# Order of loads, key rests and probabilities at the start of a causal attention, and two weight blocks placed behind query trips

## The chip, the core and the metric

The kernel runs on one core of one Trainium2 chip. The metric is device time in microseconds (us). Five engines work side by side, each on its own instruction queue: TensorE (PE in the profile, with its weight loads as PEld), VectorE (DVE), ScalarE (ACT), GpSimd (POOL) and SyncE (SP), which here only issues DMA transfers.

## What is computed

Three layers in a row, all in float32:

```python
scores = scale * np.matmul(q, k.transpose(0, 1, 3, 2))       # 2 batches, 12 heads, 448 x 64
mask = np.triu(np.ones((seq, seq), dtype=bool), k=1)
scores = np.where(mask, -1000000000.0, scores)
scores = scores - np.max(scores, axis=-1, keepdims=True)
attn = np.exp(scores)
attn = attn / (np.sum(attn, axis=-1, keepdims=True) + 1e-09)
x = np.matmul(attn, v)                                        # to (896, 768)
h = np.maximum(x @ w_in, 0.0)                                 # 768 x 2048
x = h * h @ w_out                                             # 2048 x 768
expert_idx = np.argmax(logits, axis=1)                        # 8 experts, by cosine
for e in range(E):
    h = np.maximum(x[mask] @ w1[e], 0.0)
    out[mask] = gate_w[mask, None] * (h @ w2[e])
```

## The kernel before

**Precision.** Each float32 operand of a matmul is split into a rounded half ("hi", cast to a 32-bit matmul type) and the rest ("lo", original minus hi). A product is three matmuls: hi x hi, hi x lo, lo x hi. So each key tile k becomes `kh` and `kl`, queries become `q` (both halves side by side), v becomes `vh` and `vl`, and each weight block its own pair. The helpers are `copy_on` (L60, L62: a cast on ACT, DVE or GpSimd) and `lo_of` (L67: the subtraction).

**Attention by pairs.** 24 heads are 12 pairs ("units" in the code, two heads on the 128 partitions). For a pair:

- `s_load` (L164) loads raw queries and keys, 448 KB, into one of three buffers `qk`; pair 0 in two halves. `load_v` (L174) loads v, 256 KB, into one of two buffers.
- `s_prep` (L179) makes `kh` (DVE), `kl` (GpSimd; for pair 0 DVE, by `u0`), and the scaled queries' halves: ACT rounds, DVE takes the rest (L191). For pair 0 they are written straight to where the matmul reads them. For all others they go to a buffer `qs` and from there by two DMAs of 224 KB (L202, one per head) into a block-diagonal layout `q0` or `q1`, whose zeros GpSimd wrote once. This DMA from on-chip memory to on-chip memory is called a **query trip** here. PE can't begin a pair's scores before its trip has landed.
- `s_scores` (L212): seven row blocks c of 64 query rows (both heads: 128 rows), with (c + 1) x 64 keys each; DVE takes the negative maximum, ACT the exponential with its row sum. The scores go through four PSUM banks in turn.
- `s_norm` (L246): reciprocal of the row sums on DVE (L251), then seven products p <- p x rs on GpSimd (L255).
- `s_trans` (L265): PE transposes p (L272, into `pt`), ACT rounds, DVE takes the rest. `s_pv` (L281): p times v, 24 matmuls (L290).
- `s_prep_v` (L204): v's halves; the rounding on ACT for even pairs, on GpSimd for odd, the rest on GpSimd.

**What sets the order.** The main loop (`for k in range(-3, 2 * NU + 2)`, L408) runs by half pairs: scores of the next pair, transposes of the current, products with v of the last. Its text sets PE's order, by `products` (L380), inside a manual section (`man_a`, L407, L428 to L431). GpSimd's setup (masks, zeros) is a manual section too (`zeros`, L70 to L158): it all comes ahead of any other GpSimd work. On the other engines a list scheduler of the framework places each instruction; `tc.issue_after(x)` forces an instruction behind another one in this order, as `w_load` (L106) does for the blocks of w_in, behind the load of v of pair 5 (`rpin`). Every DMA but the gathers is issued by SP, in one queue, and an issue that waits for a buffer or a result holds up all behind it. `warm` (L352) puts a few matmuls without use in front.

**After attention**: w_in and w_out in 16 blocks of 768 KB each (raw 64-bit values, converted on DVE, ACT and GpSimd in `w_load`), routing, and the experts, whose weights are loaded by index. Their code is not touched by the change.

Of the kernel before, what the change touches and what calls it, by code (L numbers as in the profile page):

```python
# [13 lines left out]
ALU = mybir.AluOpType  # L14
# [14 lines left out]
SCALE = 1.0 / 8.0  # L29
# [3 lines left out]
def f32(ap):  # L33
    return ap.bitcast(F32)
# [5 lines left out]
    turn2=[1, 3], ft0=[(0, 3), (1, 3), (2, 3), (3, 3), (4, 3)], ft1=[4], ft2=[3, 5, 6, 7], late=[(2, 5), (3, 5)], ew=[2, 4, 10, 10, 10, 12, 14], stop=0, mlo="V", xh="A", h2="A",  # L40
    wh="G", wil="G", wol="GV", warm=8, nsa=6, nwi=3, nwb=3, wo0=4, hs0=[4, 5, 8, 9], conv0=17, convs=2, pin=1,
    qsb=2, pb=2, ptb=2, qkraw=3, vraw=2, vb=2, ss=4, pts=2, pvs=2, pas=4, wsp=1,
    man=(2, 21),
    ch=(((2, 0, 1), (3,), ()), ((6,), (4, 5), ())), wn=[3, 2, 2], qh="A", qdir=1, qss=2, rpin=5, qdma="SS", kh="V",
    vh="AG", kl="G", vl="G", pth="AAAA", nrm="GGGGGGG", u0=1, order=[2, 1, 3, 0, 4], pm=1,
    pc=dict(D=(1.4, 0.8), S=(1.0, 1.0), M=(1.0, 1.7), T=(0.5, 0.65)))
# [2 lines left out]
def build(tc, qkd, vd, w_in, w_out, emb, tau, wm, cst, out, dbg_y=None):  # L49
# [56 lines left out]
    def w_load(src, f, slot, name, wh="wh", wl="wl", parts=1):  # L106

        pool, sl = slot
        hi = pool.tile([P, DM], F32R, tag=f"s{sl}h", name=name + "h")
        lo = pool.tile([P, DM], F32R, tag=f"s{sl}l", name=name + "l")  # L110
        raw = spool.tile([P, DM, 2], I32, tag="raw", name="raw")
        with tc.issue_after(last.get(("load", CFG["rpin"]), last["load"]).ins):
            DMA.dma_start(out=raw.rearrange("p a b -> p (a b)"), in_=src[:, f, :].bitcast(I32))
        w = spool.tile([P, DM], I32, tag="w24", name="w24")
        n = DM // parts
        for i in range(parts):
            x = slice(i * n, (i + 1) * n)
# [24 lines left out]
    maskf = apool.tile([P, S], F32, name="maskf")  # L142
    tri = cpool.tile([P, P], BF16, name="tri")

    for i in range(2):
        G.memset(f32(qz[i][0:D, :, 1]), 0.0)
        G.memset(f32(qz[i][D:P, :, 0]), 0.0)
        for c in range(0, NQ, 2):
            G.memset(pz[i][c][:, (c + 1) * QC:], 0.0)
        if i == 0:  # L150
            G.memset(maskf[:, 0:S - QC], 0.0)
            G.tensor_copy(maskf[:, S - QC:], mask)
    for x in vz[0] + vz[1]:
        G.memset(f32(x[:, :, 1]), 0.0)
    G.memset(tri, 1.0)
    G.affine_select(out=tri, in_=tri, pattern=[[1, P]], compare_op=ALU.is_gt, fill=0.0, base=0,
                    channel_multiplier=-1)
    zeros.__exit__(None, None, None)  # L158

    def ab(key, u):  # L160
        x = CFG[key]
        return ENG[x[units.index(u) % len(x)]]

    def s_load(u):  # L164
        b, pr = u
        qk = apool.tile([P, 2, S], F32, tag="qk", bufs=CFG["qkraw"], name="qk")
        if u == units[0]:
            for i in range(2):
                DMA.dma_start(out=qk[:, i], in_=qkd[b, pr, :, i])
        else:  # L170
            DMA.dma_start(out=qk, in_=qkd[b, pr])
        st[u] = dict(q=qk[:, 0], k=qk[:, 1])

    def load_v(u):  # L174
        b, pr = u
        st[u]["v"] = v = apool.tile([P, NB, P], F32, tag="v", bufs=CFG["vraw"], name="v")
        last["load"] = last["load", units.index(u)] = DMA.dma_start(out=v, in_=vd[b, pr])

    def s_prep(u):  # L179

        d = st[u]
        for x in ("kh", "kl"):
            d[x] = apool.tile([P, S], F32R, tag=x, bufs=CFG["qsb"], name=x)
        d["q2"] = qz[units.index(u) % len(qz)]
        first = u == units[0] and CFG["u0"]
        kh = copy_on(V if first else ab("kh", u), d["kh"], d["k"])

        def split(r, hi, lo):
            q = d["q"][r].rearrange("p (c a) -> p c a", a=QC)
            copy_on(ENG[CFG["qh"]], hi, q, scale=SCALE)  # L190
            V.scalar_tensor_tensor(out=lo, in0=q, scalar=SCALE, in1=f32(hi), op0=ALU.mult, op1=ALU.subtract)  # L191

        heads = [slice(h * D, (h + 1) * D) for h in range(2)]
        if units.index(u) < CFG["qdir"]:
# [51 lines left out]
    def s_norm(u, cs):  # L246
        d = st[u]
        rs = d["rs"]
        x = slice(COL[cs[0]], COL[cs[-1]] + 1)
        (V if units.index(u) < CFG["pm"] else G).tensor_scalar(out=rs[:, x], in0=d["sm"][:, x], scalar1=1.0e-9, scalar2=None, op0=ALU.add)  # L250
        V.reciprocal(rs[:, x], rs[:, x])  # L251
        for c in cs:
            p = d["p"][c][:, :(c + 1) * QC]
            if CFG["nrm"][c] == "G":
                G.tensor_scalar(out=p, in0=p, scalar1=rs[:, COL[c]:COL[c] + 1], scalar2=1.0, op0=ALU.mult, op1=ALU.mult)  # L255
# [92 lines left out]
    wz = apool.tile([P, 512], BF16, name="wz")
# [55 lines left out]
            mix(run, ("t", 3))  # L404
            mix(run, ("s", 3))

    man_a = tc.manual_schedule(engines={mybir.EngineType.PE})  # L407
    for k in range(-3, 2 * NU + 2):  # L408
        u, h = divmod(k, 2)
        if k == -2:  # L410
            with tc.issue_after(last["q"].ins):
                load_v(units[1])
                s_load(units[3])
        elif h == 0:
            if u + 4 < NU:
# [12 lines left out]
        if k == CFG["man"][0]:  # L428
            man_a.__enter__()
        if k == CFG["man"][1]:  # L430
# [912 lines left out]
```

## Time and profile before

| | |
|---|---|
| time, median of 3 runs (lowest, highest) | 567.44 us (566.59, 568.01) |
| time of the profiled execution | 569.09 us |
| its span, first to last instruction | 567.4 us |
| busy: PE, DVE, ACT, GpSimd | 542.6 (96%), 398.6 (70%), 288.9 (51%), 180.1 (32%) us |
| mean granted clock of TensorE | 0.986 |
| attention's share | the first 112 us or so |

A row of a timeline gives the start, the duration, the engine, the line of the code, the operation, the tile written and the tiles read (buffer numbers left out), the shape, how many of it follow one another, and in brackets how long the engine had been idle before it and for whom. The granted clock is a share of full speed.

### The profile page before, as it was taken

The page shows a single profiled execution, that of the slowest core. Times are in us where ns is not written, and L with a number is a line of the kernel's source. Part 1 is how long each engine was busy: PE and PEld are TensorE (multiplying, and loading weights), DVE is VectorE, ACT ScalarE, POOL GpSimd, SP SyncE. Part 2 cuts the span into 40 slices and gives each one's busy share as a digit, 9 for nine tenths or more (in the row PEclk, how much of TensorE's full clock was granted, in tenths as well). Part 3 has the DMA queues.
Part 4 walks back from the last instruction along what each step waited for, and adds up shares of the span by engine and source line. Part 5 has one row for each costly group of instructions (what it writes and reads, how often), then busy time and mean ns, then how long its engine had stood idle before and what let it go on. Part 6 is the DMA issues. An engine that isn't in the chain of part 4 may idle for free.

```text
span 567.4 us, 9637 instructions
## 1 busy us (share of the span) xinstructions
PE 542.6 (96%) x3429; PEld 506.5 (89%) x3430; DVE 398.6 (70%) x956; ACT 288.9 (51%) x638; POOL 180.1 (32%) x228
## 2 busy tenths in 40 slices
PE   6798899999999999999999999999999999999993
PEld 3698899988999999999899999989998898899992
DVE  6688689943977978597753556898186898783641
ACT  4687688623344433423432234741285897764641
POOL 6787588873555544221000001000301201200010
PEclk9799899999999999999999999999999999999997
DMA  6659454413454655441100006701968879874310
GB/s 169 187 136 253 110 121 100 125 62 112 123 192 137 215 161 182 162 166 57 57 28 1 29 28 245 285 28 57 328 203 280 283 252 365 283 253 155 110 53 5
DMA packets 28234, 86.52 MB, mean 152 GB/s; under 512 B 2822, under 2 KB 13062, under 8 KB 28176
## 3 DMA queue, kind: packets, MB, share of 16 engines
q1 hardware_dynamic: 26640, 79.51, 44.1%
q0 software_dynamic: 1536, 6.29, 3.1%
q8 instruction: 29, 0.48, 0.3%
q14 instruction: 29, 0.24, 0.1%
HBM read 75.24 MB, written 6.29 MB: 144 GB/s over the span
## 4 chain that ended last, share of the span: by engine, by line
PE 84%; DVE 7%; DMA 3%; ACT 3%; POOL 1%; issue 1%; SPq 0%; POOLq 0%; DVEq 0%; ACTq 0%
PE yps L581 19%; PE ops L951 10%; PE pa L314 7%; PE pa L316 7%; PE pa L315 7%; PE pv L290 5%; PE s L229 4%; PE hps L852 3%; PE pt L272 3%; PE ops L889 2%; PE ops L884 2%; DMA q<-qs 2%; PE hps L870 2%; PE hps L872 2%; PE hps L871 2%; DVE ml L67 2%
## 5 line engine op out<-in xcount | busy, mean ns | idle before, releaser
L67 DVE TENSOR_TENSOR ml<-xraw,mh 128x768 fp32r<-128x768 f32 x64 | 59.6, 956 | 10.3 <-ACT mh L60 9.8
L60 ACT ACTIVATE mh<-xraw 128x768 fp32r<-128x768 f32 x64 | 52.2, 843 | 7.6 <-PE ops L884 5.8
L951 PE MATMUL ops<-mh,act 128*128 128x384 f32 x224 | 53.5, 341 | 0.0
L229 PE MATMUL s<-kh,q 128*128 128x128 f32 (+6 forms) x168 | 45.3, 317 | 6.5 <-DMA q<-qs 5.3
L290 PE MATMUL pv<-pt,v 128*128 128x448 f32 (+7 forms) x288 | 49.0, 304 | 0.7 <-ACT pt L60 0.6
L242 ACT ACTIVATE p<-s,mn 128x192 f32<-128x192 f32 (+6 forms) x84 | 39.8, 479 | 18.1 <-DVE mn L239 12.5
L255 POOL TENSOR_SCALAR p<-p,rs 128x192 f32<-128x192 f32 (+6 forms) x84 | 43.6, 539 | 3.7 <-DVE rs L251 3.7
L122 DVE SCALAR_TENSOR_TENSOR w<-raw,w 128x768 int32<-128x768 int32 x32 | 41.9, 1310 | 0.7
L290 PEld LDWEIGHTS pv<-pt,v 128*128 128x128 f32 (+1 forms) x288 | 39.7, 169 | 2.8 <-ACT pt L60 0.8
L977 POOL DMA_INDIRECT out<-osb,fsi x10 | 9.9, 990 | 98.4 <-ACT osb L972 65.9
L239 DVE CUSTOM_DVE_ANT_0 s<-s,maskf 128x192 f32<-128x192 f32 (+6 forms) x77 | 32.4, 432 | 12.2 <-PE s L229 10.5
L229 PEld LDWEIGHTS s<-kh,q 128*128 128x128 f32 x168 | 32.1, 208 | 9.0 <-issue 5.0
L951 PEld LDWEIGHTS ops<-mh,act 128*128 128x128 f32 x224 | 39.2, 188 | 0.8
L67 DVE TENSOR_TENSOR pt<-pt 128x512 fp32r<-128x512 f32 x48 | 32.1, 683 | 9.6 <-ACT pt L60 9.6
L67 DVE TENSOR_TENSOR hs<-h,hs 128x512 fp32r<-128x512 f32 (+1 forms) x32 | 21.8, 690 | 23.1 <-ACT hs L60 22.9
L989 POOL DMA_INDIRECT xr<-ydram,fgi x10 | 10.5, 1052 | 85.4 <-DVE fsi L697 45.5
L120 DVE SCALAR_TENSOR_TENSOR w<-raw,w 128x768 int32<-128x768 int32 x32 | 37.1, 1161 | 0.7
L67 DVE TENSOR_TENSOR ml<-mraw,mh 128x768 fp32r<-128x768 f32 x32 | 29.8, 954 | 10.2 <-ACT mh L60 9.8
L320 ACT ACTIVATE relu<-pa 128x448 f32<-128x448 f32 x32 | 17.0, 539 | 34.3 <-PE pa L316 34.3
L60 ACT ACTIVATE pt<-pt 128x512 fp32r<-128x512 f32 x48 | 28.5, 600 | 11.6 <-PE pt L272 11.4
L272 PE MATMUL pt<-ident,p 128*128 128x128 f32 x192 | 29.9, 286 | 3.5 <-POOL p L255 3.0
L118 DVE TENSOR_SCALAR w<-raw 128x768 int32<-128x768 int32 x32 | 22.5, 704 | 13.8 <-POOL wi3l L67 4.3
(462 smaller groups left out, 1638.6 us busy)
## 6 DMA issues: line engine op xcount, KB each, us to landing
xraw<-in_wm SPq DMA_DIRECT2D x32, 768.0 KB, 5.8
raw<-in_w_in SPq DMA_DIRECT2D x16, 768.0 KB, 4.2
raw<-in_w_out SPq DMA_DIRECT2D x16, 768.0 KB, 4.2
mraw<-in_wm SPq DMA_DIRECT2D x16, 768.0 KB, 5.5
qk<-in_qkd SPq DMA_DIRECT2D x11, 448.0 KB, 5.7
q<-qs SPq DMA_DIRECT2D x22, 224.0 KB, 3.8
v<-in_vd SPq DMA_DIRECT2D x12, 256.0 KB, 3.3
ydram<-ysb SPq DMA_DIRECT2D x7, 384.0 KB, 2.3
```

Of the source, the lines that this page charges most:

```text
L60: return A.activation(out, in_, AF.Copy, scale=scale)
L67: return eng.tensor_tensor(out=lo, in0=x, in1=hi, op=ALU.subtract)
L122: V.scalar_tensor_tensor(out=w[:, x], in0=raw[:, x, 0], scalar=29, in1=w[:, x], op0=ALU.logical_shift_right, op1=ALU.bitwise_or)
L229: T.matmul(ss, d["q2"][:, c, :, :, x].rearrange("p a b -> p (a b)"), d[y][:, :n], start=i_ == 0, stop=i_ == 2 and not first)
L242: last["exp", units.index(u), c] = A.activation(d["p"][c][:, :n], ss, AF.Exp, bias=mn, scale=1.0 if first else -1.0, accum_out=d["sm"][:, ...
L255: G.tensor_scalar(out=p, in0=p, scalar1=rs[:, COL[c]:COL[c] + 1], scalar2=1.0, op0=ALU.mult, op1=ALU.mult)
L272: T.transpose(pt[:, o * P:(o + 1) * P], d["p"][c][:, j * P:(j + 1) * P], ident)
L290: T.matmul(d["pv"][:, j * P:S] if h else d["pv"][0:D, j * P:S], d[x][:, j, 1:3].rearrange("p a b -> p (a b)") if h else d[x][:, j, 0], pt[ ...
L314: T.matmul(ps, wh[:, c], xhi[:, kc, gs], start=(kc == 0), stop=False)
L315: T.matmul(ps, wh[:, c], xlo[:, kc, gs], start=False, stop=False)
L581: T.matmul(ps[t][c][:, :384], x, w[:, c * 384:(c + 1) * 384], start=(f == 0 and w is wh and x is hi), stop=(f == NF - 1 and x is lo))
L951: T.matmul(ps[c], x, ww[:, c * 384:(c + 1) * 384], start=(fc == 0 and x is hh and ww is wh), stop=(fc == 7 and x is hl))
```

## The change

- `hold` is new: a memset of one column of the load's target on DVE, placed behind a given instruction. The load has to follow it. v of pair 0 and the load of pair 2 are held in this way behind the cast of pair 0's keys.
- Pair 0's `kl` goes to GpSimd as all others', and the `u0` exception for keys is gone. Of pair 1, the cast `kh` comes behind the rest of its queries.
- GpSimd's setup is cut in pieces: only pair 0's zeroed query buffer stands ahead of pair 0's `kl`; the zeros of p, the mask and pair 1's query buffer come behind it, then pair 1's `kl`, then the zeros of v, more zeros of p, and `tri` (used much later).
- v of a pair is split behind the last normalization of an earlier half pair (`last["norm", ...]`), so pair 1's v comes behind pair 0's p.
- From pair 4 on a key load is issued behind the last query trip. Block f of w_in is issued behind the trip of pair 6 + f, not behind v of pair 5.
- PE's manual section opens at the start; PE's order in attention is the same as before.

```diff
-    man=(2, 21),
+    man=21,
...
+    man_a = tc.manual_schedule(engines={mybir.EngineType.PE})
+    man_a.__enter__()
...
-        with tc.issue_after(last.get(("load", CFG["rpin"]), last["load"]).ins):
+        pin = last.get(("q", 6 + f)) if src is w_in else None
+        with tc.issue_after((pin or last["load"]).ins):
             DMA.dma_start(out=raw.rearrange("p a b -> p (a b)"), in_=src[:, f, :].bitcast(I32))
...
+    def hold(x, behind):
+
+        if behind is not None:
+            with tc.issue_after(behind.ins):
+                V.memset(x, 0.0)
...
         qk = apool.tile([P, 2, S], F32, tag="qk", bufs=CFG["qkraw"], name="qk")
+        hold(qk[:, 0, 0:1], behind)
...
         st[u]["v"] = v = apool.tile([P, NB, P], F32, tag="v", bufs=CFG["vraw"], name="v")
+        hold(v[:, 0, 0:1], behind)
...
-        first = u == units[0] and CFG["u0"]
-        kh = copy_on(V if first else ab("kh", u), d["kh"], d["k"])
+        i = units.index(u)
+
+        def round_k():
+            last["kh"] = copy_on(ab("kh", u), d["kh"], d["k"])
+
+        if i != 1:
+            round_k()
...
-            split(slice(0, P), q[:, :, :, 0], q[:, :, :, 1])
+            lo = split(slice(0, P), q[:, :, :, 0], q[:, :, :, 1])
+            if i == 1:
+                with tc.issue_after(lo.ins):
+                    round_k()
...
-        lo_of(V if first else ab("kl", u), d["kl"], d["k"], f32(d["kh"]))
+        lo_of(ab("kl", u), d["kl"], d["k"], f32(d["kh"]))
...
     s_load(units[0])
     s_load(units[1])
-    load_v(units[0])
-    s_load(units[2])
     s_prep(units[0])
+    load_v(units[0], last["kh"])
+    s_load(units[2], last["kh"])
+    zero_p(0)
+    G.memset(maskf[:, 0:S - QC], 0.0)
+    G.tensor_copy(maskf[:, S - QC:], mask)
+    zero_q(1)
...
             if u + 4 < NU:
-                s_load(units[u + 4])
+                with tc.issue_after(last["q"].ins):
+                    s_load(units[u + 4])
...
         if h == 1 and 0 <= u + 1 < NU:
-            with tc.issue_after(last["max", 0, 5].ins), tc.issue_after(last["exp", 0, 5].ins):
+            with (tc.issue_after(last["max", 0, 5].ins), tc.issue_after(last["exp", 0, 5].ins),
+                  tc.issue_after(last["norm", max(k - 2, -1)].ins)):
                 s_prep_v(units[u + 1])
```

**Where instructions stand: the first DMA issues.** SP's queue from its start, before and then changed; `qk` are raw queries and keys, `q_108` and `q_110` take pair 1's trip, `q_107` and `q_109` pair 2's.

```order
L169 DMA qk<-in_qkd 128x448 x2
L171 DMA qk<-in_qkd 128x896
L177 DMA v<-in_vd 128x512
L171 DMA qk<-in_qkd 128x896
L202 DMA q_108<-qs 64x7x128 x2
L177 DMA v<-in_vd 128x512
L171 DMA qk<-in_qkd 128x896 x2
L202 DMA q_107<-qs 64x7x128 x2
```

```order
L174 DMA qk<-in_qkd 128x448 x2
L176 DMA qk<-in_qkd 128x896
L183 DMA v<-in_vd 128x512
L176 DMA qk<-in_qkd 128x896
L216 DMA q_110<-qs 64x7x128 x2
L183 DMA v<-in_vd 128x512
L176 DMA qk<-in_qkd 128x896
L216 DMA q_109<-qs 64x7x128 x2
L176 DMA qk<-in_qkd 128x896
```

The first five rows stand in the same order; the third and fourth (v of pair 0, load of pair 2) now wait for DVE's memsets. Pair 4's key load has gone behind pair 2's trip.

**GpSimd, behind its setup.** Before and then changed; `p_113` to `p_119` and `p_115` to `p_121` are pair 0's seven p, `v_111` and `v_113` pair 1's v.

```order
L62 CAST v_111<-v 128x4x2x64
L255 TENSOR_SCALAR p_115<-p_115,rs 128x192
L255 TENSOR_SCALAR p_113<-p_113,rs 128x64
L255 TENSOR_SCALAR p_114<-p_114,rs 128x128
L255 TENSOR_SCALAR p_116<-p_116,rs 128x256
L67 TENSOR_TENSOR v_112<-v,v_111 128x4x2x64
L67 TENSOR_TENSOR kl<-qk,kh 128x448
L255 TENSOR_SCALAR p_119<-p_119,rs 128x448
L255 TENSOR_SCALAR p_117<-p_117,rs 128x320
L255 TENSOR_SCALAR p_118<-p_118,rs 128x384
```

```order
L269 TENSOR_SCALAR p_117<-p_117,rs 128x192
L269 TENSOR_SCALAR p_115<-p_115,rs 128x64
L269 TENSOR_SCALAR p_116<-p_116,rs 128x128
L269 TENSOR_SCALAR p_118<-p_118,rs 128x256
L456 AFFINE_SELECT tri<-tri 128x128
L67 TENSOR_TENSOR kl<-qk,kh 128x448
L269 TENSOR_SCALAR p_121<-p_121,rs 128x448
L269 TENSOR_SCALAR p_119<-p_119,rs 128x320
L269 TENSOR_SCALAR p_120<-p_120,rs 128x384
L62 CAST v_113<-v 128x4x2x64
L264 TENSOR_SCALAR rs<-sm 128x4
L67 TENSOR_TENSOR v_114<-v,v_113 128x4x2x64
```

Pair 1's v, cast and rest, has gone from ahead of and between pair 0's p to behind them.

**SP at the first weight blocks.** Before and then changed; `raw` are blocks of w_in, and in both the first row is v of pair 6 or the trip of pair 6.

```order
L177 DMA v<-in_vd 128x512
L113 DMA raw<-in_w_in 128x1536 x2
L202 DMA q_107<-qs 64x7x128 x2
L171 DMA qk<-in_qkd 128x896
L177 DMA v<-in_vd 128x512
L202 DMA q_108<-qs 64x7x128 x2
```

```order
L216 DMA q_109<-qs 64x7x128 x2
L176 DMA qk<-in_qkd 128x896
L116 DMA raw<-in_w_in 128x1536
L183 DMA v<-in_vd 128x512
L216 DMA q_110<-qs 64x7x128 x2
L176 DMA qk<-in_qkd 128x896
L116 DMA raw<-in_w_in 128x1536
L183 DMA v<-in_vd 128x512
```

The two blocks stood together ahead of pair 6's trip (`q_107`); now one stands behind that trip (`q_109`) and its key load, the other behind the next pair's.

## Rows read from the trace of the kernel before

**Rows 1.** Busy by stage: stretch, length, PE, PEld, DVE, ACT, POOL, PEclk, DMA share, GB/s.

```profile
2.00:7.00 5.00, 3.83 (x13) 1.43 (x10) 3.69 (x5) 1.50 (x4) 4.78 (x13) 1.00 0.91 293
22.00:28.00 6.00, 6.00 (x29) 5.76 (x29) 3.79 (x13) 4.41 (x14) 3.21 (x8) 0.53 0.43 115
28.00:30.00 2.00, 2.00 (x12) 1.87 (x11) 1.78 (x6) 1.21 (x3) 1.45 (x3) 0.70 1.12 202
36.00:44.00 8.00, 8.00 (x66) 7.79 (x65) 7.36 (x25) 7.14 (x24) 7.28 (x13) 1.00 0.58 146
59.00:64.00 5.00, 4.68 (x28) 4.71 (x29) 2.32 (x10) 2.06 (x8) 0.95 (x3) 0.66 0.24 46
```

**Rows 2.** Who PE waited for: us in total, times, longest.

```profile
PE pt L272 <- POOL p L255: 3.0, 3, 2.3
```

**Rows 3.** Timeline of PE, first 60 us.

```profile
6.94 0.74 PE L229 MATMUL s<-kl,q 128*128 128x192 f32 x4 [1.00 <-DVE kl L67]
...
13.85 0.34 PE L229 MATMUL s<-kh,q 128*128 128x192 f32 x1 [1.23 <-DMA q<-qs]
...
21.27 0.33 PE L272 MATMUL pt<-ident,p 128*128 128x128 f32 x1 [2.30 <-POOL p L255]
...
27.37 1.05 PE L272 MATMUL pt<-ident,p 128*128 128x128 f32 x4
...
48.40 0.34 PE L229 MATMUL s<-kh,q 128*128 128x192 f32 x1 [1.01 <-DMA q<-qs]
...
59.32 0.34 PE L229 MATMUL s<-kh,q 128*128 128x192 f32 x1 [3.12 <-DMA q<-qs]
```

**Rows 4.** Timeline of GpSimd (POOL), 8 to 25 us.

```profile
8.73 1.43 POOL L67 TENSOR_TENSOR kl<-qk,kh 128x448 fp32r<-128x448 f32 x1 [0.33 <-DVE kh L62]
...
15.07 0.61 POOL L62 CAST v<-v 128x512 fp32r<-128x512 f32 x1 [4.67 <-DMA v<-in_vd]
...
17.59 1.29 POOL L67 TENSOR_TENSOR v<-v,v 128x512 fp32r<-128x512 f32 x1
18.83 1.14 POOL L67 TENSOR_TENSOR kl<-qk,kh 128x448 fp32r<-128x448 f32 x1
19.94 1.84 POOL L255 TENSOR_SCALAR p<-p,rs 128x448 f32<-128x448 f32 x3
...
23.30 1.52 POOL L255 TENSOR_SCALAR p<-p,rs 128x192 f32<-128x192 f32 x4
```

**Rows 5.** Timeline of VectorE (DVE): casts of keys, and pair 1's query rest.

```profile
3.96 1.05 DVE L62 CAST kh<-qk 128x448 fp32r<-128x448 f32 x1 [0.82 <-DMA qk<-in_qkd]
...
8.56 0.61 DVE L191 SCALAR_TENSOR_TENSOR qs<-qk,qs 128x448 fp32r<-128x448 f32 x1
...
31.71 0.39 DVE L62 CAST kh<-qk 128x448 fp32r<-128x448 f32 x1
```

**Rows 6.** DMAs, us to landing at the end; issued at 1.72, 9.95, 13.1, 43.0, 51.6.

```profile
qk<-in_qkd SPq DMA_DIRECT2D x1, 448.0 KB, 5.7
...
q<-qs SPq DMA_DIRECT2D x1, 224.0 KB, 3.8
...
q<-qs SPq DMA_DIRECT2D x1, 224.0 KB, 7.0
...
q<-qs SPq DMA_DIRECT2D x1, 224.0 KB, 5.3
...
q<-qs SPq DMA_DIRECT2D x2, 224.0 KB, 7.6
```

**Rows 7.** Timeline of SP's DMA issues: start, time to issue.

```profile
1.72 0.43 SPq L171 DMA_DIRECT2D qk<-in_qkd  x1
...
9.20 1.37 SPq L202 DMA_DIRECT2D q<-qs  x2
...
42.33 1.27 SPq L202 DMA_DIRECT2D q<-qs  x2
...
46.41 0.91 SPq L113 DMA_DIRECT2D raw<-in_w_in  x2
```

More of the change, by code (lines that the diff above doesn't have):

```diff
@@ L143, in build, with zero_q, zero_p @@
     tri = cpool.tile([P, P], BF16, name="tri")
-    for i in range(2):
+    def zero_q(i):
         G.memset(f32(qz[i][0:D, :, 1]), 0.0)
         G.memset(f32(qz[i][D:P, :, 0]), 0.0)
+    def zero_p(i):
         for c in range(0, NQ, 2):
             G.memset(pz[i][c][:, (c + 1) * QC:], 0.0)
[L150 to L158, printed above, removed]
+    zero_q(0)
     def ab(key, u):
@@ L162, in ab, with s_load @@
         return ENG[x[units.index(u) % len(x)]]
-    def s_load(u):
+    def hold(x, behind):
+        if behind is not None:
+            with tc.issue_after(behind.ins):
+                V.memset(x, 0.0)
+    def s_load(u, behind=None):
         b, pr = u
         qk = apool.tile([P, 2, S], F32, tag="qk", bufs=CFG["qkraw"], name="qk")
+        hold(qk[:, 0, 0:1], behind)
         if u == units[0]:
@@ L172, in s_load, with load_v @@
         st[u] = dict(q=qk[:, 0], k=qk[:, 1])
-    def load_v(u):
+    def load_v(u, behind=None):
         b, pr = u
         st[u]["v"] = v = apool.tile([P, NB, P], F32, tag="v", bufs=CFG["vraw"], name="v")
+        hold(v[:, 0, 0:1], behind)
         last["load"] = last["load", units.index(u)] = DMA.dma_start(out=v, in_=vd[b, pr])
@@ L190, in split @@
             copy_on(ENG[CFG["qh"]], hi, q, scale=SCALE)
-            V.scalar_tensor_tensor(out=lo, in0=q, scalar=SCALE, in1=f32(hi), op0=ALU.mult, op1=ALU.subtract)
+            return V.scalar_tensor_tensor(out=lo, in0=q, scalar=SCALE, in1=f32(hi), op0=ALU.mult, op1=ALU.subtract)
         heads = [slice(h * D, (h + 1) * D) for h in range(2)]
-        if units.index(u) < CFG["qdir"]:
-            with tc.issue_after(kh.ins):
+        if i < CFG["qdir"]:
+            with tc.issue_after(last["kh"].ins):
                 for h, r in enumerate(heads):
@@ L199, in s_prep @@
             q = apool.tile([P, NQ, QC, 2], F32R, tag="qs", bufs=CFG["qss"], name="qs")
-            split(slice(0, P), q[:, :, :, 0], q[:, :, :, 1])
+            lo = split(slice(0, P), q[:, :, :, 0], q[:, :, :, 1])
+            if i == 1:
+                with tc.issue_after(lo.ins):
+                    round_k()
             for h, r in enumerate(heads):
-                last["q"] = ENG[CFG["qdma"][h]].dma_start(out=f32(d["q2"][r, :, h]), in_=f32(q[r]))
-        lo_of(V if first else ab("kl", u), d["kl"], d["k"], f32(d["kh"]))
+                last["q"] = last["q", i] = ENG[CFG["qdma"][h]].dma_start(out=f32(d["q2"][r, :, h]), in_=f32(q[r]))
+        lo_of(ab("kl", u), d["kl"], d["k"], f32(d["kh"]))
     def s_prep_v(u):
@@ L254, in s_norm @@
             if CFG["nrm"][c] == "G":
-                G.tensor_scalar(out=p, in0=p, scalar1=rs[:, COL[c]:COL[c] + 1], scalar2=1.0, op0=ALU.mult, op1=ALU.mult)
+                last["norm"] = G.tensor_scalar(out=p, in0=p, scalar1=rs[:, COL[c]:COL[c] + 1], scalar2=1.0, op0=ALU.mult,
+                                               op1=ALU.mult)
             else:
@@ L339, in norm_at @@
             s_norm(units[u], sum(CFG["ch"][k % 2], ()))
+            last["norm", k] = last["norm"]
     s_load(units[0])
     s_load(units[1])
-    load_v(units[0])
-    s_load(units[2])
     s_prep(units[0])
+    load_v(units[0], last["kh"])
[4 more added lines that the diff above has]
+    zero_q(1)
     wz = apool.tile([P, 512], BF16, name="wz")
@@ L405, in products @@
             mix(run, ("s", 3))
-    man_a = tc.manual_schedule(engines={mybir.EngineType.PE})
     for k in range(-3, 2 * NU + 2):
@@ L427, in build @@
                 w_in_load()
[L428 to L430 removed]
+        if k == CFG["man"]:
             man_a.__exit__(None, None, None)
@@ L433, in build @@
             s_prep(units[1])
+            for x in vz[0] + vz[1]:
+                G.memset(f32(x[:, :, 1]), 0.0)
+            zero_p(1)
+            G.memset(tri, 1.0)
+            G.affine_select(out=tri, in_=tri, pattern=[[1, P]], compare_op=ALU.is_gt, fill=0.0, base=0,
+                            channel_multiplier=-1)
+            zeros.__exit__(None, None, None)
         norm_at(k)
```

## The prediction

> **What bounds the kernel now.** I read the busy times by stage first, then the list of who waited for whom, then the timelines of TensorE (PE), GpSimd (POOL), VectorE (DVE) and the DMA issues in the first 64 us. PE is busy 96% of the span, and 8.00 of 8.00 us in the steady stretch 36 to 44 [rows 1], where DVE, ScalarE (ACT) and GpSimd are each about 90% busy. So the time is PE's own work, its idle gaps, and stretches at the lower clock. Two causes make the gaps that the change can reach: normalized probabilities p from GpSimd, 3.0 us [rows 2], and query trips (q<-qs), 1.23 + 1.01 + 3.12 = 5.4 us [rows 3], all before 60 us. The reader should see six PE rows [rows 3]: 1.00 us at 6.94 for the rest of the first keys (kl), 1.23 at 13.85 for pair 1's trip, 2.30 at 21.27 for pair 0's last p, 1.01 at 48.40 and 3.12 at 59.32 for the trips of pairs 5 and 6, and at 27.37 the first transposes of pair 1. After the two longest gaps the granted clock is 0.53 over 22 to 28, 0.70 over 28 to 30 and 0.66 over 59 to 64 [rows 1]: between the 1.2 GHz level (0.50) and the 2.4 GHz level (1.00). It had not fallen after the gaps of 1.23 and 1.01 us. Lost there: 6 x 0.47 + 2 x 0.30 = 3.4 us, and 5 x 0.34 = 1.7 us.
>
> PE's order in attention does not change at all, so every microsecond that PE starts sooner at 64 us is carried to the end, if no other engine takes over.
>
> **First keys.** Pair 0's keys are rounded on DVE at 3.96 in 1.05 us, beside GpSimd's memsets; a later pair's, undisturbed, takes 0.39 [rows 5]. In the new order GpSimd has only zeroed pair 0's queries by then (till about 3.95) and waits for the cast, so I take 0.4: done at 4.35. The rest kl moves from DVE, where it stood behind the two query rests, to GpSimd: 1.14 to 1.43 us by [rows 4], done at 5.5 to 5.8. The DVE queue loses that operation and gains two memsets of one column. No row has such a memset: between 0 and the 0.39 of a whole cast I take 0.1, as a column is 1/448 of it; they stand between the two query rests, so DVE ends those at about 5.9. PE's pass with kl starts near 5.7 instead of 6.94. That is 1.0 us for PE there, but the wait for pair 1's trip swallows it, so I don't add it.
>
> A rule speaks against this move. The kl on GpSimd at 8.73 took 1.43 us while DVE's query rest ran from 8.56, against 1.14 at 18.83 [rows 4, 5], so 0.29 us were lost. The Trainium skill, SBUF — State Buffer, section "Who interferes with whom", says that a VectorE instruction with two SBUF inputs and a GpSimd one that reads SBUF block each other wholly, the first one in front. By that rule kl would run to 5.5 and both query rests after it, to 7.0, so pair 1's trip would be issued 1.2 us later than I take it; as the loads in front of that trip bound its landing anyhow, the sum would stay within 0.3 us.
>
> **Pair 1's trip.** Its raw keys and queries (448 KB, issued 1.72) land after 5.7 us, at 7.4, with v of pair 0 (256 KB) and pair 2's load (448 KB) issued right behind [rows 6, 7]. These two now wait for a memset behind the first keys' cast, so they are issued at about 5.15 and 5.6. Pair 0's 448 KB landed at 3.96; at the 293 GB/s of 2 to 7 us [rows 1] the next 448 KB need 1.5 us: landing at 5.4, bounds 5.4 and 7.4 (no gain). ACT then rounds the queries (0.63), DVE takes the rest (0.61 [rows 5], now ahead of the key cast, not behind it), and the trip is issued at 6.5 to 7.3 instead of 9.20 [rows 7]. But now the 704 KB held back flow in front of it. Before, the trip's second half landed 3.8 us after its issue [rows 6], 4.55 us after the first half's. Some 300 KB ahead cost another 1.0: 6.55 + 4.55 + 1.0 = 12.1, against 13.75. Gain 1.6 us; bounds 0.5 (load no sooner) and 2.2 (trip alone).
>
> **Probabilities of pair 0.** GpSimd waits 4.67 us for pair 1's v at 15.07, casts it (0.61), normalizes four p (from 15.68 to 17.59, 1.9), takes the rest of v (1.29) and pair 2's kl (1.14), and only then normalizes the last three p (1.84), done at 21.8 [rows 4]; PE waits for these. In the new order v's cast and rest stand behind the last p. I place GpSimd's queue by the same durations: first kl to 5.8, memsets, pair 1's kl (1.43), the other memsets. Before, all its setup behind pair 0's zeros, with one kl in it, ended at 10.4 (15.07 - 4.67); the added kl and the 0.4 us of waiting make that 11.7 to 12.0, without the select behind it. Then four p to 13.7, the small select, pair 2's kl to 15.1, three p to 16.9. PE, 1.6 us sooner at pair 1's scores, is 1.6 + 2.3 + 0.5 = 4.4 sooner at the last ones, at about 17: no wait left, or a short one. So the 3.0 us of [rows 2] go.
>
> What is late next is GpSimd itself: v's cast (0.61) to 17.5, a reciprocal's input 17.8, v's rest 19.05, pair 3's kl 20.2, four p of pair 1 (1.5 to 1.9) 22.0. PE alone would be at pair 1's transposes sooner: the 6.1 us from 21.27 to 27.37, less 2.5 for the clock and 0.2 of waiting, end at 20.5. So they start at 22.0 with GpSimd, against 27.37: 5.4 us. What the slow clock cost behind 27.37 (0.63 x 0.47 + 2 x 0.30) adds 0.9. **Front: 6.3 us**; bounds 3.4 (the rival on GpSimd, below) and 7.8 (PE alone).
>
> **Weight blocks.** Two 768 KB blocks of w_in are issued together at 46.41 [rows 7]. The second half of pair 5's trip, in flight then, lands after 5.3 us and pair 6's after 7.6, where pair 1's took 3.8 [rows 6]. Now each block stands alone behind the trip and key load of pairs 6 and 7. What stands behind a trip costs it little (that 3.8 us had v and two key loads behind), what stands in front costs much (7.0 us for pair 2's trip, behind two key loads). A trip has some 5 us from its first issue until PE wants it (48.40 - 1.01 - 42.33 [rows 3, 7]). In the steady 8 us the DMA engines are busy 58% with a pair's own transfers [rows 1]; the 3.4 us left hold a block of 768 KB, 2.6 us at 293 GB/s. So 3.12 + 1.7 = **4.8 us** go at 59.32, and of the 1.01 at 48.40 I take **0.9**; bounds 0 and 1.01, as that trip was slow already before the blocks could flow.
>
> **What is added.** Later v loads wait for GpSimd's later rest; they are wanted a pair later. The constraint that a key load waits for the trip before it puts pair 4's key load behind pair 2's trip, which helps that trip. Pair 2's trip, 1.5 us sooner and with one key load less in front, lands near 17.5 (20.1 before: [rows 6] has 7.0 us, from 13.1), and PE wants it near 18: little room. In the expert stages a few matmuls of the second product move ahead or behind by two to six places; nothing waits there now, so 0, bounds -0.5 and 0.5. For small new waits on engines that are 90% busy I take off **1.0** (bounds 0 and 2).
>
> **Sum.** 6.3 + 0.9 + 4.8 - 1.0 = 11.0 us. The profiled execution itself took 569.09 us (span 567.4), 1.65 above the median of the three runs, 567.44; from the median, **556.4 us**. The bounds together: -7.8 - 1.0 - 4.8 - 0.5 to -3.4 - 0 - 4.8 + 2.5, so 553.3 to 561.7.
>
> **Rivals.** *The first loads land no sooner.* For it: pair 0's own keys landed at 3.96 [rows 5] with three loads queued behind. Then pair 1's trip lands at 13.3, the last p of pair 0 end at 17.8, pair 1's at 22.8: 0.8 us less, 557.2. The Trainium skill, DMA: Bandwidth & Descriptors, "Queues, rings and completion order", says that each DMA engine takes one issuing engine's descriptors in ring order. By that rule loads behind could not slow the one ahead and the holding back would be empty; the 5.7 us for the second load, about as late as all 1600 KB, speak against it here. *GpSimd becomes the pace* in the front: its queue has a new kl and, if DVE blocks it, four p of pair 1 end at 24.8 as before. The transposes then start at 24.9, a gain of 2.5 + 0.9 = 3.4 there: 559.3. *The blocks hit more trips* (slower): a block two microseconds behind a trip rides with that trip's tail and with the next trip, so the trips of pairs 6, 7 and 8 all come as late as pair 6's did. Three times 4.8 against a gain of 6.3 + 5.7 is 2.4 more than before: 569.8. It decides where a trip's second half lands over 5 us after its first issue, and reaches the full price at 8.3. Against it: the 3.8 us with three loads behind. *No change* in sum, if PE's saved time is given back at the start of the first dense product, where DVE and GpSimd convert weights (567); against it, that stretch follows attention's own order.
>
> **Chances.** Forecast 0.65, loads no sooner 0.15, GpSimd's pace 0.13, blocks 0.04, no change 0.03. The range, 553.0 to 562.0, holds the first three. A difference of 0.3% (1.7 us) is about what can be told from no change: faster 0.93, same 0.03, slower 0.04.
>
> **What would show it.** PE's row of pair 1's first score near 12, no wait for p near 17, granted clock 1.00 over the whole front, the first product with v (28.08 before) near 22.5; no wait for a trip near 40 to 55, and phase A's first matmul about 11 us sooner. I am wrong if a new wait over 2 us stands before 64 us, or if the clock falls there again.

## The result and the profile after

The changed kernel takes 561.91 us (median of 7 runs, 559.99 to 564.03), the kernel before 567.29 beside it (566.11 to 568.40): ratio 0.9912, interval 0.9886 to 0.9937. It is faster by 5.4 us; the forecast was 11.0 us and 556.4 us. The profiled execution took 561.91 (span 560.2), its median.

Busy by stage, changed kernel, columns as in [rows 1]:

```profile
22.00:28.00 6.00, 5.02 (x33) 4.04 (x32) 4.97 (x16) 4.40 (x15) 5.46 (x14) 1.00 0.71 179
28.00:30.00 2.00, 1.95 (x18) 1.98 (x19) 1.36 (x7) 1.68 (x6) 1.03 (x2) 1.00 0.01 4
36.00:44.00 8.00, 8.00 (x67) 7.80 (x67) 6.95 (x24) 6.68 (x22) 5.76 (x10) 1.00 0.55 145
59.00:64.00 5.00, 4.23 (x34) 4.04 (x35) 3.29 (x12) 4.49 (x15) 4.20 (x7) 1.00 0.69 218
```

The granted clock is 1.00 (2.4 GHz) wherever it had been 0.53 to 0.70. Who PE waited for, 0 to 106 us (total, times, longest), the list of [rows 2]:

```profile
PE s L243 <- ACT p L256: 2.0, 3, 0.9
PE s L243 <- DMA q<-qs: 1.8, 2, 1.1
PE pt L287 <- DVE pt L67: 1.1, 3, 0.5
```

No wait for GpSimd's p is left. Timeline of PE, the places of [rows 3] and three later pairs:

```profile
12.26 0.33 PE L243 MATMUL s<-kh,q 128*128 128x192 f32 x1
...
13.50 0.31 PE L243 MATMUL s<-kh,q 128*128 128x64 f32 x1 [0.67 <-ACT p L256]
...
28.05 0.34 PE L243 MATMUL s<-kh,q 128*128 128x192 f32 x1 [0.91 <-ACT p L256]
...
43.16 0.34 PE L243 MATMUL s<-kh,q 128*128 128x192 f32 x1
...
50.72 0.34 PE L243 MATMUL s<-kh,q 128*128 128x192 f32 x1
...
59.62 0.34 PE L243 MATMUL s<-kh,q 128*128 128x192 f32 x1 [1.09 <-DMA q<-qs]
...
76.00 0.33 PE L243 MATMUL s<-kh,q 128*128 128x192 f32 x1 [0.67 <-DMA q<-qs]
...
92.03 0.33 PE L243 MATMUL s<-kh,q 128*128 128x192 f32 x1 [0.42 <-ACT p L256]
```

Pairs 5 and 6 (43.16, 50.72) wait no more. Pairs 3, 7, 9 and 11 do, 0.91 + 1.09 + 0.67 + 0.42 = 3.1 us. The first and last of these stand under ACT, whose exponential ended just then (27.90 and 91.97), as did the trips issued at 22.11 and 86.13 (landed at 27.96 and 91.94). It was the trips: in run e10_pe_shift60 below, where they land sooner, the same two scores start before that exponential has ended. Landing of the two halves of pair 7's trip, and of the first half of pair 8's, whose second half is missing from the trace (issue to landing, us):

```profile
DMA to landing us min/median/max: 5.0/5.2/5.5
...
DMA to landing us min/median/max: 3.3/3.3/3.3
```

VectorE and GpSimd in the front, against [rows 4, 5]:

```profile
4.99 1.42 DVE L202 SCALAR_TENSOR_TENSOR q<-qk,q 64x448 fp32r<-64x448 f32 x1
...
9.85 1.57 DVE L264 TENSOR_SCALAR rs<-sm 128x4 f32<-128x4 f32 x1 [0.86 <-ACT p L256]
...
9.84 1.07 POOL L453 MEMSET v<- 128x256 f32 x4
10.85 0.41 POOL L154 MEMSET p<- 128x64 f32 x4
```

The second query rest of pair 0 took 1.42 us beside GpSimd's kl (4.54 to 5.92), against 0.61 for the first; the addition `rs` took 1.57 us beside memsets; where nothing else runs it takes 0.17 (run e5_zeros_later).

**What the four late trips have in common.** The trace's DMA packets hold 29 of 16,384 bytes in a queue of kind "instruction"; between two of them PE starts 255 instructions in the median (weight loads and matmuls together). The Trainium skill, Runtime: NRT & Kernel Launch, "Instruction fetch mechanics", says that an engine's program is refilled in blocks of 16 KiB, 256 instructions, through a DMA queue of its own, and that the cost is mostly hidden; the count agrees, the cost here doesn't. These packets during attention, in the changed kernel:

```
packet starts, took   trip in flight (first issue)   its second half landed after
24.86  0.88           pair 3 (22.11)                 5.2
44.20  0.97           none                           -
56.25  0.93           pair 7 (53.37)                 5.5
72.66  0.92           pair 9 (69.84)                 5.4
89.40  0.96           pair 11 (86.13)                5.2
no packet             pairs 4, 5, 6                  3.8, 3.8, 3.8
no packet             pairs 8, 10                    not in the trace (first halves 3.3, 3.3)
```

Of pairs 8 and 10 the last packet starts 3.7 and 3.6 us after the first issue, as of pairs 4 to 6 (3.7), so they were on time. Behind pair 11's trip no other large transfer was in flight. From 87.5 to 89.5 us, 65 to 133 packets of 512 bytes start in each quarter of a microsecond; from 90.0 to 91.7 it is 28 in all, one after another, the first at 90.34, as the block ends (90.36). A half of a trip, 224 KB, is 448 such packets, 28 for each of 16 DMA engines: just one engine's share was left. **Theory A**: PE's instruction block delays one DMA engine's share of a trip in flight, so the trip lands 1.4 to 1.7 us late. Rivals: **B**, what is queued behind a trip slows it; **C**, other engines' pace takes the gain back.

### The profile page after: what moved, and what is told of

Its sections match the earlier page's. It is cut to its first block, busy times and chain, and to the rows that moved or that the text cites. A ratio compares the mean times of both kernels' runs of the same rounds, so it can differ in the third digit from the quotient of the medians.

```text
span 560.2 us, 9639 instructions
## 1 busy us (share of the span) xinstructions
PE 541.2 (97%) x3429; PEld 504.4 (90%) x3430; DVE 397.6 (71%) x957; ACT 288.3 (51%) x638; POOL 183.4 (33%) x229
## 3 DMA queue, kind: packets, MB, share of 16 engines
q0 software_dynamic: 1536, 6.29, 3.1%
HBM read 75.24 MB, written 6.29 MB: 146 GB/s over the span
## 4 chain that ended last, share of the span: by engine, by line
PE 83%; DVE 6%; ACT 4%; DMA 3%; issue 2%; POOL 1%; SPq 0%; POOLq 0%; ACTq 0%; DVEq 0%
PE yps L607 20%; PE ops L977 9%; PE pa L329 7%; PE pa L331 7%; PE pa L330 7%; PE pv L305 5%; PE s L243 4%; PE hps L878 3%; PE ops L915 3%; PE pt L287 2%; PE ops L910 2%; PE hps L896 2%; PE hps L898 2%; PE hps L897 2%; DVE ml L67 2%
## 5 line engine op out<-in xcount | busy, mean ns | idle before, releaser
L305 PE MATMUL pv<-pt,v 128*128 128x448 f32 (+7 forms) x288 | 47.0, 297 | 0.7 <-ACT pt L60 0.6
L269 POOL TENSOR_SCALAR p<-p,rs 128x192 f32<-128x192 f32 (+6 forms) x84 | 44.9, 552 | 4.9 <-DVE rs L265 4.5
L305 PEld LDWEIGHTS pv<-pt,v 128*128 128x128 f32 (+1 forms) x288 | 38.2, 163 | 2.7 <-ACT pt L60 0.8
L1015 POOL DMA_INDIRECT xr<-ydram,egi x2 | 2.3, 1149 | 84.0 <-DVE esi L723 83.7
```

The costliest lines, as they stand in the source:

```text
L269: last["norm"] = G.tensor_scalar(out=p, in0=p, scalar1=rs[:, COL[c]:COL[c] + 1], scalar2=1.0, op0=ALU.mult, op1=ALU.mult)
L305: T.matmul(d["pv"][:, j * P:S] if h else d["pv"][0:D, j * P:S], d[x][:, j, 1:3].rearrange("p a b -> p (a b)") if h else d[x][:, j, 0], pt[ ...
```

## The experiments

### Each part alone

In the kernel before, the new pin of the weight blocks only:

```diff
-        with tc.issue_after(last.get(("load", CFG["rpin"]), last["load"]).ins):
+        pin = last.get(("q", 6 + f)) if src is w_in else None
+        with tc.issue_after((pin or last["load"]).ins):
...
```

> The kernel before, with one part of the change alone: each of the first two weight blocks waits for the query trip of its own pair (pairs 6 and 7) instead of both for pair 5's v load. The prediction's terms for this part are 0.9 + 4.8 = 5.7 us, so 561.6 from 567.3. Theory A (PE's instruction block of 16 KB, one packet on one DMA engine, is what makes single trips late): pair 5's trip keeps its wait of about 1 us, since an instruction block came at 45.06 us, inside its flight, before any weight block; only pair 6's 3.12 us and the 1.7 us of clock behind it go, 4.8 us, and a later trip loses 0.5 to 1.1 us where an instruction block meets it: 562.5 to 563.5. Rival B (what stands behind a trip slows it): pairs 6 and 7, each with a block behind, wait 1 us or more each, pair 5 waits no more: 563 to 564.

563.35 us, 0.9911 (0.9878 to 0.9943). Pair 5's trip still landed after 5.3 us, with a block at 42.92 inside its flight and no weight block near; so did pair 7's (5.5, block 59.28), pair 9's (4.7, 75.48) and pair 11's (5.0, 91.47). Pairs 6 and 8 took 3.8. That is A; B had pair 6 late. The time alone lies in the intervals of both.

In the changed kernel, the old pin back:

```diff
-        pin = last.get(("q", 6 + f)) if src is w_in else None
-        with tc.issue_after((pin or last["load"]).ins):
+        with tc.issue_after(last.get(("load", CFG["rpin"]), last["load"]).ins):
```

> The changed kernel with the weight blocks put back where they were, both behind pair 5's v load: the front of the change alone. The prediction's terms for it are 6.3 - 1.0 = 5.3 us: 562.0. Theory A: 4.0 to 5.0 us by pair 3's first score, the same waits of 1.0 and 3.1 us as before at pairs 5 and 6 and the lower clock behind them, so 562.5 to 563.5. Rival C (GpSimd and DVE, with more to do for pair 0 and 1, hand the gain back pair by pair behind the front): the gain at pair 4 is under 3 us and the time over 564.5.

566.22 us, 0.9978 (0.9956 to 1.0000). Its profiled execution follows A's expectation: pair 4's first score at 35.54 (39.59 in the first profile of before), pair 6's trip lands after 6.8 us and PE waits 2.8. But the median gains 1.1 us only; the time by itself is what rival C had (over 564.5). The parts add up (3.9 + 1.1 = 5.0, against 5.4), and the front is the one that was far too large; the last section of experiments shows against what.

### The instruction blocks moved

In the changed kernel, 60 more PE instructions ahead of the first pairs, in fillers whose result is not used:

```diff
-            T.matmul(wp, wz[:, 0:P], wz, start=True, stop=True)
+            for _ in range(3): T.matmul(wp[:, 0:170], wz[:, 0:P], wz[:, 0:170], start=True, stop=True)
```

> The changed kernel, with each of the 15 filler matmuls of 512 columns on zeros in front of and between the first scores written as three of 170 columns: 60 more instructions in PE's stream (a weight load and a matmul each), the same columns, nothing else. PE reads its program in blocks of some 256 instructions, about 16.7 us of attention, so each later block is fetched some 4 us sooner. In the changed kernel the blocks came 2.7 to 3.3 us behind the first issue of the trips of pairs 3, 7, 9 and 11, and these four landed 5.2 to 5.5 us after their issue, all others 3.3 to 3.8 (pair 2's 4.8). Theory A: the blocks now come about a microsecond ahead of those trips, all of them land in 3.3 to 3.9 us, PE's waits of 0.91, 1.09, 0.67 and 0.42 us are gone: 3.1 us less, 558.8. Rival B (key loads and weight blocks behind the trip, or the tile of the odd pairs): the same four trips are late, 561.9 within 0.5. Rival C (engines' pace): the trips may land sooner but PE waits for p, pt or s in place, over 561.

559.45 us, 0.9850 (0.9821 to 0.9880). Timeline of PE in this run, pairs 3, 7, 9 and 11:

```profile
26.77 0.34 PE L243 MATMUL s<-kh,q 128*128 128x192 f32 x1
...
57.03 0.34 PE L243 MATMUL s<-kh,q 128*128 128x192 f32 x1
...
72.83 0.34 PE L243 MATMUL s<-kh,q 128*128 128x192 f32 x1
...
88.39 0.34 PE L243 MATMUL s<-kh,q 128*128 128x192 f32 x1
```

No wait stands at any of them, and every trip of pairs 3 to 11 lands within 3.9 us. Pair 11 starts 3.6 us sooner than in the change (88.39 against 92.03), the four waits and a little. The blocks moved further than worked out (17.73, 35.29, 52.28, 65.22, 80.65), and the one at 17.73 met pair 2's trip (5.5 us), which has room. B falls, as nothing behind a trip was moved. C falls, as no engine's work was moved but PE's fillers, and PE is now busy 16.00 of 16.00 us from 28 to 44 us.

Still more instructions, so that the blocks should meet the trips of even pairs:

```diff
-    def warm(n):
+    def warm(n, m=5):
...
-            T.matmul(wp, wz[:, 0:P], wz, start=True, stop=True)
+            for _ in range(m): T.matmul(wp[:, 0:512 // m], wz[:, 0:P], wz[:, 0:512 // m], start=True, stop=True)
...
-    warm(CFG["warm"])
+    warm(7, 4)
```

> The changed kernel with still more and shorter fillers: the first 7 in four of 128 columns, the later 7 in five of 102, 96 instructions more in PE's stream than in the change and 36 more than in run e10_pe_shift60. The blocks come some 2.5 us sooner than in e10 (there 35.29, 52.28, 65.22, 80.65, beside trips of 36.96, 52.11, 59.20, 67.59, 74.77 and 83.15). Theory A: they fall into the flights of the pairs of even number: two or three of the trips of pairs 4, 6, 8 and 10 land over 4.8 us after their issue, none of pairs 3, 7, 9 and 11 does, and the time is back at 560.5 to 562. Rival (run e10 was quicker because of the fillers themselves, or the tiles of odd pairs): no trip of pairs 3 to 11 over 4.2 us, 559.4 again, or the odd ones late again.

559.94 us (558.42 to 562.25), 0.9864 (0.9823 to 0.9906); the profiled execution took 562.25. Late are pair 4 (5.7 us, block 2.76 behind the issue) and pair 6 (5.1, 2.89); the odd pairs take 3.7 to 3.8. The trips follow the blocks, as A has it; the median is half a microsecond below its interval.

The changed kernel once more, with no edit:

> The changed kernel, unchanged, once more, with a second profile. Theory A: every trip of pairs 3 to 11 that lands over 4.5 us after its issue has a 16 KB packet in its flight, and no other; 561 to 563. If the order of four late trips (3, 7, 9, 11) is chance, others are late here.

561.69 us, 0.9898 (0.9856 to 0.9940). Late: pairs 3, 5, 7, 9 and 11 (5.1, 5.3, 5.5, 5.3, 5.2), with blocks at 24.76, 40.80, 57.21, 73.64 and 90.29, and no other trip. The traces lack the landing of some second halves, but none lacks packets, so over all 13 traces and the trips of pairs 3 to 11 I take the start of a trip's last packet, counted from its first issue (its first packet starts at 1.25 us). Of 29 trips whose packets a block overlapped, 25 took 4.7 to 5.4 us; the other four met the block at one end only (begun 0.5 to 0.8 or 3.6 us behind the issue) and took 3.7 to 4.4. Of 88 without, 80 took 3.6 to 3.8, five 4.1 to 4.5, and three 5.4 to 7.6: those are pair 6's with both weight blocks in front. Why the five are up to 0.9 us late was not tried.

Trips issued sooner in the changed kernel:

```diff
-            x = (0, 3) if u < 0 else (u + 1, 5)
+            x = (0, 3) if u < 0 else (u + 1, 4)
```

> The changed kernel, where a pair's keys and queries are prepared behind the score of chunk 4 instead of chunk 5 of the pair two ahead: on ACT and DVE the query rounding and its rest stand one or two places further ahead, and each trip is issued some 0.7 to 1.2 us sooner against the place where PE wants it. Theory A: a trip still takes up to 5.5 us where an instruction block meets it, but the room grows from 5.2 to about 6 us: the four waits, 3.1 us in sum, shrink to under 0.8 and the time is 559 to 560, less what the probabilities lose that now stand behind the query rounding on ACT. Rival C (engines' pace): the moved work delays exponentials and transposes by as much, 561.5 to 563.

561.74 us, 0.9885 (0.9857 to 0.9914): inconclusive. From pair 2's first score to pair 11's PE needs 71.3 us (20.55 to 91.86) instead of 72.9, but pair 2 began 1.5 us later, while in this execution the clock fell to 0.79 over 14 to 22 us (8 x 0.21 = 1.7 us). Two trips met a block and landed after 5.4 us, pair 5's and pair 9's, and PE waited for neither: the added room holds a late trip.

### The front's parts, on the kernel without late trips

The next four start from run e10_pe_shift60, 559.45 us, and keep its fillers. GpSimd's later zeros behind the first four p:

```diff
-            for x in vz[0] + vz[1]:
...
         norm_at(k)
+        if k == -2:
+            for x in vz[0] + vz[1]:
```

> The kernel of run e10_pe_shift60 (the change with the fillers in three, 559.45), with GpSimd's later zeros (v, second p, tri) moved behind the first four p of pair 0. In the change these ran from 9.84 to 11.39 and DVE's small addition rs of 128x4, 0.17 us where nothing else runs, took 1.57 beside them; the 448-column maximum behind it on DVE started only at 12.07, its exponential at 12.72, and PE waited 0.7 for it at 13.5. If GpSimd's memsets are what stretches rs: rs takes under 0.3 us, the 448-column maximum starts at 10.7 to 11.0, PE's wait of 0.7 goes and the first four p end 1.3 us sooner; 0.7 us less at pair 1's scores, of which the zeros, 1.3 us now between the first four p and the last three, may take back some: 558.6 to 559.3. Rival (rs is late because of ACT's sums, not because of GpSimd): rs keeps over 1 us and nothing changes but the later p of pair 0: 559.5 to 560.5.

559.61 us, 0.9848 (0.9813 to 0.9882). DVE's timeline in this run:

```profile
9.78 0.17 DVE L264 TENSOR_SCALAR rs<-sm 128x4 f32<-128x4 f32 x1 [0.78 <-ACT p L256]
...
12.04 2.00 DVE L62 CAST kh<-qk 128x448 fp32r<-128x448 f32 x1 [0.18 <-PE s L249]
```

`rs` is back at 0.17, so the memsets had stretched it; but now they (12.24 to 13.78) stretch the key cast to 2.00 (0.39 elsewhere), and nothing is won. The Trainium skill, SBUF — State Buffer, "Who interferes with whom", says that a cast or a tensor_scalar can take the ports that VectorE shares with GpSimd, and that the other then waits wholly; both rows agree (the addition ended at 11.42 in the change, GpSimd's memsets at 11.39).

The two loads no longer held back:

```diff
-    load_v(units[0], last["kh"])
-    s_load(units[2], last["kh"])
+    load_v(units[0])
+    s_load(units[2])
```

> The kernel of run e10_pe_shift60 without the two one-column memsets that hold back v of pair 0 and pair 2's load: both loads are issued at once again. If loads that stand behind share the DMA engines with pair 1's first load, as the prediction had it: pair 1's keys and queries land 5.5 us or more after their issue instead of 4.6, its trip is issued at 8.3 to 8.6 and not 7.4, pair 1's first score starts at 13 or later instead of 12.11, and the time is 0.8 to 1.5 us longer: 560.3 to 561. Rival (a load is served in the order of issue, so the holding back is empty): 4.6 us, first score at 12.1, 559.4 or a little less, as v and pair 2's keys come sooner.

561.18 us, 0.9870 (0.9834 to 0.9906). Pair 1's keys and queries land 5.2 us after their issue, not 4.4, its trip is issued at 8.23, not 7.44, and its first score starts at 12.93, not 12.11: the loads behind do slow the one ahead. But pair 2 starts 0.25 us later and pair 11 only 0.2 (88.58 against 88.39). The rest of the 1.7 us lies behind attention in that execution, so the times don't settle what holding is worth; by the traces it is 0.2.

Pair 0's kl back on VectorE:

```diff
-        lo_of(ab("kl", u), d["kl"], d["k"], f32(d["kh"]))
+        lo_of(V if i == 0 else ab("kl", u), d["kl"], d["k"], f32(d["kh"]))
```

> The kernel of run e10_pe_shift60 with the first keys' rest (kl of pair 0) back on DVE, behind the two query rests. If that rest on GpSimd blocks DVE's second query rest (1.42 us instead of 0.64): the query rest falls to 0.65, kl on DVE ends at about 6.4 instead of 5.92, PE's kl pass starts 0.5 later, and pair 1's trip, whose query rest waits for its load, is issued at the same 7.4 to 7.6; GpSimd gets its zeros done 1.4 us sooner, ahead of rs: 559.0 to 559.6, no difference to 559.45 that can be told. If moving it to GpSimd is what brings PE's first pass forward, as the prediction had it, and that counts: first scores 1 us later, 560 to 560.5.

559.49 us, 0.9844 (0.9810 to 0.9879): the move of pair 0's kl is worth nothing. DVE's second query rest is 0.62 us again, although GpSimd's memsets run beside it (5.05 to 6.78): memsets don't stretch every operation on VectorE.

```profile
5.64 0.62 DVE L202 SCALAR_TENSOR_TENSOR q<-qk,q 64x448 fp32r<-64x448 f32 x1
```

Pair 1's v split ahead of pair 0's last p again:

```diff
...
-                  tc.issue_after(last["norm", max(k - 2, -1)].ins)):
...
```

> The kernel of run e10_pe_shift60 without the wait of the v split for the last p: GpSimd casts v of pair 1 before pair 0's first four p and takes its rest (1.29 us) before pair 2's kl and the last three p, as in the kernel before. The prediction gave the order of GpSimd 3.0 us of waits for p and 3.4 us of lower clock together. If that order is what removed them: waits for p from GpSimd of 1 to 2 us come back ahead of 22 us and the transposes of pair 1 start over 1 us later than 22.8; without a fall of the clock 560.5 to 562, with one at 22 to 28 us up to 564. Rival (the sooner landing of v and trips alone took the waits away): under 0.5 us of such waits, 559 to 560.

560.75 us, 0.9879 (0.9844 to 0.9915). Stage 14 to 22 us and PE's waits, 0 to 115 us, in this run:

```profile
14.00:22.00 8.00, 7.21 (x41) 6.25 (x40) 5.07 (x21) 5.77 (x20) 7.84 (x13) 0.79 0.76 194
...
PE pt L287 <- DVE pt L67: 2.1, 3, 1.4
PE s L243 <- DMA q<-qs: 0.9, 1, 0.9
PE pt L287 <- POOL p L269: 0.8, 2, 0.5
```

Pair 2's first score comes at 21.20 instead of 18.93, pair 11's 2.3 us later, the median 1.3. Of the 2.3 us, 1.7 (8 x 0.21) are the lower clock of this execution, which fell in the same stretch in run e4_trips_sooner too, with the new order. So GpSimd's order does count, but for 0.6 us by this trace and 1.3 by the medians, not for 3.0 + 3.4: with the sooner loads and trips alone the waits for p are already 0.8.

### The kernel before, looked at again

> The kernel before, unchanged, looked at once more, since its first profiled execution took 569.09 us against a median of 567.3. If the long wait for pair 6's trip and the clock behind it are the same in every execution: pair 6's first score waits 3 us, phase A's first matmul starts at 113 to 114 us, total 568.5 to 569.5. If that execution had bad luck in trips and clock: PE's waits in attention differ by 1 to 3 us from the first execution's, and the total with them.

This execution took 563.97 us, 5.1 less than the one that the prediction was read from, with the same code. Its rows:

```profile
22.00:28.00 6.00, 5.66 (x39) 4.94 (x38) 5.23 (x18) 5.11 (x17) 4.18 (x10) 1.00 0.47 120
28.00:30.00 2.00, 2.00 (x21) 1.96 (x20) 1.67 (x6) 1.46 (x4) 2.00 (x5) 1.00 0.91 253
59.00:64.00 5.00, 4.51 (x36) 4.14 (x33) 4.34 (x14) 3.52 (x11) 3.53 (x6) 1.00 0.85 218
...
29.23 0.34 PE L229 MATMUL s<-kh,q 128*128 128x192 f32 x1
...
55.28 0.33 PE L229 MATMUL s<-kh,q 128*128 128x192 f32 x1 [1.85 <-ACT pt L60]
```

Against [rows 1, 3]: the clock stayed at 1.00 in all three stretches, pair 6's wait was 1.85 and not 3.12 (its trip took 6.3 us, not 7.6), pair 3 began at 29.23 instead of 32.03. A third trace with the old front, run e1_blocks_only's, lies between:

```profile
22.00:28.00 6.00, 6.00 (x36) 5.80 (x35) 4.71 (x17) 5.33 (x17) 3.76 (x9) 0.72 0.51 132
...
29.89 0.34 PE L230 MATMUL s<-kh,q 128*128 128x192 f32 x1
```

The clock's fall over 22 to 30 us is no fixed part of the kernel before. But a clock that falls somewhere is its rule, and this execution the exception: it is faster than any of 35 further times of the kernel before, taken beside these runs (564.49 to 570.90, median 567.94). Their mean granted clock over the whole program is 0.980 to 0.990 in 26 and 0.992 to 0.998 in nine; it was 0.986 in the first profile and is 0.995 here, and 0.992 to 0.997 in 11 runs of the changed kernel. Where it falls, only profiled executions show; what decides whether it falls, and how much of the 5.4 us is clock, was not tried.

## Why the prediction was off

The time lies in the range (553.0 to 562.0), 5.5 us above the forecast. Point by point, by PE's rows of the changed kernel against the first profile of before (the sum is of the five rows behind the first, which is part of the front):

| term | predicted | measured |
|---|---|---|
| pair 1's first score | 1.6 | 1.6 (13.85 to 12.26) |
| front, clock included | 6.3 | 4.9 (4.0 at pair 3's first score, and its wait of 0.9) |
| pair 5's trip | 0.9 | 1.2 |
| pair 6's trip | 3.1 | 3.4 |
| clock behind it | 1.7 | 1.3 |
| new waits | -1.0 | -3.1 |
| at the end of attention | 11.0 | 7.7 by this sum; 7.55 by phase A's dense run (113.35 to 105.80) |
| end of the program | 11.0 | 7.2 in spans, 5.4 in medians |

Phase A is the first dense product behind attention, x @ w_in. The first row of its dense run, before and then changed:

```profile
113.35 0.39 PE L316 MATMUL pa<-xhi,wi0l 128*128 128x448 f32 x1
...
105.80 0.39 PE L331 MATMUL pa<-xhi,wi0l 128*128 128x448 f32 x1
```

- **Right**: which waits go, the clock at 1.00 over the front, the landing of pair 2's trip (17.67, predicted 17.5), and that two weight blocks ahead of pair 6's trip were its delay.
- **Right by luck**: the landing of pair 1's trip (12.12, predicted 12.1). The load in front landed at 6.29 and not at 5.4, and the trip was issued at 7.63 and not at 6.55; but the loads held back, put at 1.0, cost it nothing (second half 3.7 us, 3.8 before). The two errors cancel. Pair 5's 0.9 is luck too: its wait went because no instruction block met its trip in this execution; in run e12_after_again, the same kernel, it is 0.88 again. And PE waits for p no more, but GpSimd's new order has the smaller part in that: without it the waits are 0.8 of 3.0 us (run e8_v_first).
- **Failed step 1, "For small new waits on engines that are 90% busy I take off 1.0".** It is 3.1, outside the bounds of 0 to 2, and of another kind: PE's instruction block in a trip's flight. The step before it, that a trip has some 5 us and is hurt only by what stands in front, counted loads alone. The wait at 48.40 [rows 3], given to the weight blocks with "that trip was slow already before the blocks could flow" as a doubt, was such a case too: a block started at 45.06. Run e10_pe_shift60, without late trips, got 2.5 us of median back and PE to pair 11 3.6 us sooner.
- **Failed step 2, the front's 6.3 us and the clock's 1.7 taken "from the median".** 3.4 + 1.7 us of slow clock were read from an execution that took 1.65 us more than the median, and priced as if present in full in every run. The traces gain 7.2 us and the medians 5.4; the 1.8 us between are that execution's distance from 567.29. Pair 3's first score, 4.0 us sooner against it, is 1.2 and 1.8 us sooner (28.05) against the other two traces of the old front (29.23, 29.89), and in medians the front is worth 1.1 us alone and 1.4 on top of the blocks (563.35 to 561.91). Lower clock was not absent from the other runs of the kernel before, most of which show as low a mean as the first profile; where in them it fell stays open.
- **Smaller**: the front gained 4.9 us by the traces, not 6.3; transposes of pair 1 start at 22.79, not 22.0. The 1.57 us of `rs` kept GpSimd's first p late; taking that away moved the stall to the key cast. The rule on shared ports, weighed at 0.3 us for kl, held there, and showed again where the working had not looked, beside memsets.
- The rivals didn't occur: the load in front landed after 4.6 us and not 5.7, moving GpSimd's zeros or kl away won nothing (559.61 and 559.49, against 559.45), and the weight blocks hit no further trip.

The version without late trips, run e10_pe_shift60, beats both kernels: 559.45 us, against 561.91 and 567.29.

## What to carry to other kernels

List the DMA packets of the instruction streams before a short transfer is called late because of its neighbours; here PE's program has a fixed length per round, its blocks met the same transfer nearly every second round, and some instructions more ahead of the loop moved them. Read a gain that hangs on the granted clock from two executions at least, and take it off the execution in which it was seen. A cast or a small addition on VectorE beside GpSimd is costed by what GpSimd runs then, memsets included, not by its own size.

## What the runs showed of the hardware that was not expected

- A 16 KB block of PE's instructions takes 0.88 to 1.4 us as one packet. A 224 KB on-chip transfer that it meets midway lands 4.7 to 5.7 us after its issue instead of some 3.8; behind the block that met pair 11's, 28 packets, one DMA engine's share, were left to move.
- On VectorE beside GpSimd memsets, an addition of 128x4 took 1.57 us (0.17 alone) and a cast of 128x448 2.00 (0.39), but a query rest of 64x448 0.62, as elsewhere.
- The same program's granted clock over 22 to 28 us was 0.53 in one execution and 1.00 in another.
